# Attention product in halves of TensorE's rows, and a new order of the first units, in a fused attention and mixture-of-depths kernel

## The chip, the cores and the metric

The kernel runs on one core of a Trainium2 chip. A core has TensorE (PE: matmuls, with weight loads as instructions of their own), VectorE (DVE), ScalarE (ACT), GpSimd (POOL) and SyncE (SP), each with its own instruction queue that it works through in order, and 16 DMA engines that move data between HBM, the chip's large memory, and SBUF, the core's own. Matmul results land in PSUM. The engines wait for each other by semaphores. The metric is the device time of one execution in microseconds (us).

## The reference

Inputs are `q`, `k`, `v` of shape (8, 8, 576, 64): 8 batches, 8 heads, 576 positions, head size 64, all float32.

```python
q_s = softmax(q, axis=-1)                       # over the head size
k_s = softmax(k, axis=2)                        # over the positions
kv  = einsum('bhsd,bhse->bhde', k_s, v)         # 64 x 64 for each head
x   = einsum('bhsd,bhde->bhse', q_s, kv)        # then heads side by side: (8, 576, 512)
for b in range(8):
    scores = x[b] @ w_gate                      # one number for each position
    top = argpartition(-scores, 128)[:128]      # the 128 best positions
    xe = x[b, top]
    y  = maximum(xe @ w1, 0) @ w2               # w1: 512 x 1024, w2: 1024 x 512
    out[b] = x[b]
    out[b, top] = xe + sigmoid(scores[top])[:, None] * y
```

So each batch has an attention part over all positions and an MLP over its 128 best ones, and the MLP of a batch can't start before the whole batch's scores are known.

## The kernel before

**Units.** Work is cut into 16 units `s`: a batch has two, of four heads each. The 576 positions lie as 64 groups of 9 over the partitions: a partition holds 5 positions (`R = 5`) or 4 and a zeroed one. For one unit the steps are

- `load`: k, v and q from HBM, six transfers on SP's queue into one of three sets of buffers
- `k_exp`, `q_exp`: exponentials on ScalarE (L195, L202); `v_copy`: v next to a column of ones (L205), on GpSimd in the first units, else on VectorE
- `kv_mm`: k^T v with the column sums of k, 20 matmuls in two column halves of the array (L215); `kv_out`: its reciprocals on VectorE (L224), the copy of the result on ScalarE (L226), and on VectorE one more column, kv times the gate weights `wg` (L228, L229), so that the product gives the score as well
- `q_t`: transposes of exp(q) on TensorE (L239), scaled with the reciprocals as they leave PSUM (L242, "eviction") on ScalarE
- `x_mm`: the product of q and kv (L253); `x_out`: divided by q's sums on VectorE (L266, L267), with the score column (L269); `x_store`: the unit's rows of `out` to HBM on SP's queue

After the second unit of a batch come `score` (L283 to L294, VectorE and GpSimd), `score_row` (the scores as a row, transposed on TensorE, L302, copied by ScalarE, L305 and L307), five `compare` on VectorE (L315, the rank of each position), `pick` (the index list: L335 on VectorE, L339 on TensorE, L343 to L345, and an indirect DMA on GpSimd that gathers the rows `xr`, L347), `gate` (the sigmoid), `turn` (the rows transposed on TensorE, L368, and copied by ScalarE, L370), `mlp1` in eight pieces (L382, each fourth followed by a Relu on ScalarE, L385), `mlp2` in eight pieces (L392) and `finish` (L400, and the indirect store L401).

Each fp32 matmul, not a transpose, stands in the trace as two records with a weight load each: `x_mm` of a unit, 40 matmuls, as 80.

**Order.** The kernel writes down the order itself: the program order is each engine's order. The first four units (`EARLY = 4`) run in a loop of their own, without an MLP; `fill(n)` puts n matmuls of no use in, and `WARM = 20` such matmuls stand at the start. At its end are `gate` and `turn` of batch 0. In each of its steps the `kv_mm` of the next unit is done, so `kv_mm(4)` is too. From step 4 on a step has one unit's attention and, four units behind, half a batch's MLP: eight `pieces` of `mlp1` in even steps and of `mlp2` in odd ones, two after the transposes, one after the next unit's `kv_mm`, four later, and one last. In odd steps `pick` comes after the first two pieces and `turn` before the last one.

The four matmuls of one head pair and position take a quarter of the array each, 64 rows by 64 columns:

```python
QUARTERS = (0, 0), (1, 1), (0, 1), (1, 0)
for h, c in QUARTERS:
    nc.tensor.matmul(out=x[part(c), h, r * C:(r + 1) * C], lhsT=qT[part(h), i, r, c],
                     rhs=kv_w[u % 2][part(h), i], start=True, stop=True)
```

Of the kernel before, what the change touches and what calls it, by code (L numbers as in the profile page):

```python
# [17 lines left out]
def kernel(  # L18
# [24 lines left out]
    R = 5  # L43
# [11 lines left out]
    UP = 2.0 ** 24  # L55
    TINY = 2.0 ** -126
    NV = 5
    WARM = 20
    assert S == 64 * (R + N2) and D == 64 and DM == H * D and DM == 512 and H % 4 == 0
    assert 1 < capacity < S and KF == 8 and NQ == 2  # L60
    assert B * S <= 32 * 256
# [12 lines left out]

    def bank(tag, bufs):
        return ps.tile([P, 512], F32, tag=tag, name=tag, bufs=bufs)


    QUARTERS = (0, 0), (1, 1), (0, 1), (1, 0)

    def part(i):
        return slice(64 * i, 64 * i + 64)
# [38 lines left out]

    wg = const.tile([P, NQ, 2, D], F32, name="wg")
    for h in range(2):
        nc.scalar.dma_start(out=wg[part(h)].rearrange("p a i d -> p (a i) d"),
                            in_=bass.AP(tensor=moe_w_gate.tensor, offset=moe_w_gate.offset + h * D,
                                        ap=[[0, 64], [2 * D, 2 * NQ], [1, D]]))
    warm = const.tile([P, 1], F32, name="warm")
# [65 lines left out]
    def k_exp(u):  # L193
        ke = at.tile([P, 4, R, D], F32, tag="ke", name="ke")
        nc.scalar.activation(out=ke, in_=raw["k"][u % LD], func=AF.Exp)  # L195
        st["ke", u] = ke

    def q_exp(u, i):
        if i == 0:
            st["qe", u] = at.tile([P, 2, R, 2, D], F32, tag="qe", name="qe")  # L200
        qr = raw["q"][u % LD].rearrange("p (i h) r d -> p i r h d", i=2)
        nc.scalar.activation(out=st["qe", u][:, i], in_=qr[:, i], func=AF.Exp)  # L202

    def v_copy(u, engine=nc.vector):
        engine.tensor_copy(out=v_ones[u % 2][:, :, :, :D], in_=raw["v"][u % LD])  # L205
# [22 lines left out]
        nc.vector.tensor_mul(prod, kv[:, :, :D], wg[:, qd])  # L228
        nc.vector.reduce_sum(out=kw[:, :, D + 1], in_=prod, axis=AX.X)  # L229

    def q_t(u, i):

        if i == 0:
            st["qT", u] = at.tile([P, 2, R, 2, D], F32, tag="qT", name="qT")
        qe = st["qe", u] if i == 0 else st.pop(("qe", u))
        t_ps = ps.tile([P, 2, 512], F32, tag="x", name="x", bufs=2)
        for r in range(R):
            for a in range(2):
                nc.tensor.transpose(out=t_ps[:, a, r * 64:(r + 1) * 64],  # L239
                                    in_=qe[part(a), i, r].rearrange("p h d -> p (h d)"),  # L240
                                    identity=ident[part(a), part(a)])
        nc.scalar.activation(out=st["qT", u][:, i].rearrange("p r a c -> p a r c"),  # L242
                             in_=t_ps[:, :, :R * 64].rearrange("p a (r c) -> p a r c", r=R),
                             func=AF.Copy, scale=krec[:, u, i:i + 1])

    def x_mm(u, i):


        qT = st["qT", u] if i == 0 else st.pop(("qT", u))
        x = ps.tile([P, 2, 512], F32, tag="x", name="x", bufs=2)  # L250
        for r in range(R):
            for h, c in QUARTERS:
                nc.tensor.matmul(out=x[part(c), h, r * C:(r + 1) * C], lhsT=qT[part(h), i, r, c],  # L253
                                 rhs=kv_w[u % 2][part(h), i], start=True, stop=True)
        st["x", u, i] = x

    xs, sr = {}, {}

    def x_out(u, i):
        b, qd = units[u]  # L260
        if qd == 0 and i == 0:
            xs[b] = xp.tile([P, R, NQ, 2, 2, D], F32, tag="xs", name="xs")
            sr[b] = md.tile([P, NQ * 2, G], F32, tag="sr", name="sr")
        x = st.pop(("x", u, i))[:, :, :R * C].rearrange("p h (r c) -> p h r c", r=R)
        rec = qrec[:, u, i].rearrange("p (h r) -> p h r", h=2)
        nc.vector.reciprocal(out=rec, in_=x[:, :, :, D])  # L266
        nc.vector.tensor_mul(xs[b][:, :, qd, i].rearrange("p r h d -> p h r d"), x[:, :, :, :D],  # L267
                             rec.to_broadcast([P, 2, R, D]))
        nc.vector.tensor_mul(sr[b][:, 2 * qd + i].rearrange("p (h r) -> p h r", h=2), x[:, :, :, D + 1], rec)  # L269

    def x_store(u):
        b, qd = units[u]
# [7 lines left out]
    def score(b, up=2):  # L280

        raw_s = s_all[:, b]
        nc.vector.reduce_sum(out=raw_s, in_=sr.pop(b).rearrange("p a (h r) -> p r a h", h=2),  # L283
                             axis=AX.XY)
        s = md.tile([P, R], F32, tag="s", name="s")
        nc.vector.tensor_mul(s, raw_s, valid_r[:, up])
        nc.vector.tensor_add(s, s, valid_r[:, 1])
        st["s", b] = s

        left = md.tile([P, R], F32, tag="left", name="left")  # L290
        for c in range(2, NV):
            nc.gpsimd.tensor_copy(out=vals[:, b, :, c], in_=raw_s if c == 2 else left)
            if c < NV - 1:
                nc.gpsimd.tensor_sub(left, raw_s if c == 2 else left, vals[:, b, :, c])  # L294
# [15 lines left out]
    def compare(b, r):  # L310

        if r == 0:
            st["rank", b] = md.tile([P, R], F32, tag="rank", name="rank")
        junk = md.tile([P, RP], BF16, tag="junk", name="junk", bufs=1)
        nc.vector.scalar_tensor_tensor(junk, st["srow", b], st["s", b][:, r:r + 1], not_before[:, r],  # L315
                                       op0=OP.subtract, op1=OP.is_ge, accum_out=st["rank", b][:, r:r + 1])
# [185 lines left out]
    def fill(n):  # L502

        junk_ps = bank("mm", 2)
        for _ in range(n):
            nc.tensor.matmul(out=junk_ps, lhsT=ones_b[:, :P], rhs=ones_b, start=True, stop=True)
# [12 lines left out]

    for s in range(EARLY):  # L520
        q_t(s, 0)
        q_t(s, 1)
        k_exp(s + 1)
        v_copy(s + 1, nc.gpsimd)
        fill(2)
        x_mm(s, 0)
        x_mm(s, 1)
        fill(2)
        if s == 2:
            kv_mm(s + 1)  # L530
            q_exp(s + 1, 0)
            fill(3)
            pick(0)
            x_out(s, 0)
            kv_out(s + 1)
            x_out(s, 1)
            x_store(s)
            q_exp(s + 1, 1)
        else:
            x_out(s, 0)  # L540
            x_out(s, 1)
            x_store(s)
            if s == 1:
                score(0)
            kv_mm(s + 1)
            q_exp(s + 1, 0)
            kv_out(s + 1)
            if s == 1:
                score_row(0)
                for r in range(R):  # L550
                    compare(0, r)
            q_exp(s + 1, 1)
            if s == 3:
                score(1)
        fill(2)
        if s == 0:
            load_w1(0)
            load_w1(1)
        elif s == 1:
            load_w1(2)  # L560
            load_w1(3)
            load(4, "kvq")
            load(5, "kvq")
        else:
            load_w2(s - 2)
            load(s + 4, "kvq")
    each(gate, 0)
    each(turn, 0)

    number = None  # L570
    for s in range(EARLY, NU + LAG):

        mlp_b, odd = divmod(s - LAG, 2)
        piece = mlp2 if odd else mlp1
        f_next = 0

        def pieces(n):
            nonlocal f_next
            for _ in range(n):
                each(piece, mlp_b, f_next)  # L580
                f_next += 1

        here = s < NU
        after = s + 1 < NU
        last = s == NU - 1
        ends = s // 2 if here and odd else None
        compared = s // 2 - 1 if here and not odd else None
        chosen = (s - 3) // 2 if here and odd else B - 1 if s == NU else None
        if here:
            q_t(s, 0)  # L590
            q_t(s, 1)
        if after:
            v_copy(s + 1)
            k_exp(s + 1)
        pieces(2)
        if chosen is not None:
            pick(chosen)
        if here:
            x_mm(s, 0)
            x_mm(s, 1)  # L600
            x_out(s, 0)
            x_out(s, 1)
            x_store(s)
        if last:
            score(ends)
        if after:
            kv_and_exp(s + 1)
        if s + 4 < NU:
            load(s + 4, "kvq")
        pieces(1)  # L610
        if last:
            compared = ends
        if compared is not None:
            score_row(compared)
            for r in range(R):
                compare(compared, r)
        if chosen is not None:
            each(gate, chosen)
        if ends is not None and not last:
            score(ends)  # L620
        pieces(4)
        if odd and mlp_b + 1 < B:
            each(turn, mlp_b + 1)
        pieces(1)
        if odd:
            each(finish, mlp_b)
        if s == NU:
            number = sums_in_range()
# [28 lines left out]
```

## Time and profile before

| | |
|---|---|
| device time, three runs | 218.83, 220.24, 220.49 us, median 220.24 |
| span of the profiled execution | 216.0 us |
| PE busy | 197.5 us (91%) |
| weight loads (PEld) busy | 147.2 us (68%) |
| DVE, ACT, POOL busy | 54%, 41%, 16% |
| L253, the product | 1280 matmul records of 64x64 in 16 units |
| DMA from 9 to 42 us | busy 1.07 of its 16 engines' time, 370 GB/s |
| DMA from 86 to 108 us | 0.73, 232 GB/s |
| first matmul of the MLP | 42.64 us |

A row of the timeline gives start, length, engine, line, operation, what is written from what, the count of merged instructions, and in brackets the idle time before them with what ended it. PE's busy time counts filler as work, and matmuls overlap, so lengths of single ones can't be added up; the distance from one group's start to the next group's start is what a group costs. [...]A wait counts only on the engine that the end of the run hangs on.

### The profile page before, as it was taken

How to read it: one execution, taken by the hardware profiler on the slowest of the kernel's cores; microseconds unless marked ns; L12 is line 12 of the kernel's file. 1: busy time of each engine (PE TensorE's matmuls, PEld its weight loads, DVE VectorE, ACT ScalarE, POOL GpSimd, SP SyncE). 2: the span in 40 equal slices, each digit the busy share in tenths (PEclk: the TensorE clock that was granted, in tenths of full speed). 3: DMA queues.
4: the chain of work that ended last, by engine and by line, in shares of the span. 5: the costliest groups of instructions: out<-in, count | busy, mean ns of one | idle time of the engine just before them, and what ended most of it. 6: DMA issues, size and time to landing. Idle time of an engine off the chain costs nothing. (4 is left out here: it accounts for less than half of the span.)

```text
span 216.0 us, 7090 instructions
## 1 busy us (share of the span) xinstructions
PE 197.5 (91%) x3040; PEld 147.2 (68%) x3040; DVE 116.2 (54%) x359; ACT 88.6 (41%) x146; POOL 34.4 (16%) x78
## 2 busy tenths in 40 slices
PE   5987595999999999999999999999999989999960
PEld 2464462799749975897679776996599548749620
DVE  6552595668726774477626872596358665501010
ACT  2386374763626471746265443536263311211100
POOL 6022402300112012200320023001120112101010
PEclk9999999999999999999999999999999999999996
DMA  5999999999999997958594949421313041101001
GB/s 179 299 356 358 375 398 369 362 392 377 377 384 381 375 344 249 314 157 283 171 320 154 313 133 303 161 82 49 113 52 109 7 156 52 49 3 52 5 5 52
DMA packets 39335, 46.81 MB, mean 217 GB/s; under 512 B 2944, under 2 KB 36736, under 8 KB 39296
## 3 DMA queue, kind: packets, MB, share of 16 engines
q1 hardware_dynamic: 36928, 41.36, 56.4%
q0 software_dynamic: 1280, 4.20, 5.7%
q10 hardware_dynamic: 1088, 0.72, 1.1%
q8 instruction: 26, 0.43, 0.8%
q14 instruction: 13, 0.11, 0.2%
HBM read 34.73 MB, written 11.53 MB: 214 GB/s over the span
## 5 line engine op out<-in xcount | busy, mean ns | idle before, releaser
L382 PE MATMUL mm<-xT,w 128*128 128x128 f32 x512 | 62.1, 278 | 0.0
L382 PEld LDWEIGHTS mm<-xT,w 128*128 128x128 f32 x512 | 58.8, 192 | 2.3 <-ACT xT L370 1.5
L392 PE MATMUL mm<-w,hT 128*128 128x512 f32 x128 | 59.9, 603 | 0.0
L315 DVE SCALAR_TENSOR_TENSOR junk<-srow,s,not_before 128x576 bf16<-128x576 f32 x40 | 32.8, 819 | 8.3 <-ACT srow L307 7.2
L392 PEld LDWEIGHTS mm<-w,hT 128*128 128x128 f32 x128 | 22.5, 190 | 21.2 <-issue 20.4
L267 DVE TENSOR_TENSOR xs<-x,qrec 128x640 f32<-128x640 f32 x32 | 26.4, 825 | 1.1
L242 ACT ACTIVATE qT<-x,krec 128x640 f32<-128x640 f32 x32 | 23.9, 792 | 6.2 <-PE x L239 6.1
L400 DVE SCALAR_TENSOR_TENSOR o<-mm,g,xr 128x512 f32<-128x512 f32 x8 | 6.0, 751 | 37.7 <-PE mm L392 37.7
L202 ACT ACTIVATE qe<-q 128x640 f32<-128x640 f32 x32 | 23.6, 739 | 3.0 <-DMA q<-in_q_dram 2.8
L215 PE MATMUL tp<-v_ones,ke 128*64 128x65 f32 x640 | 22.6, 224 | 2.3 <-issue 2.1
L215 PEld LDWEIGHTS tp<-v_ones,ke 128*64 128x64 f32 x640 | 20.3, 137 | 5.3 <-issue 3.0
L253 PE MATMUL x<-kv_w,qT 64*64 64x66 f32 x1280 | 22.4, 221 | 0.0
L347 POOL DMA_INDIRECT xr<-out_dram,idx x8 | 8.0, 996 | 88.8 <-DVE qrec L266 72.6
L253 PEld LDWEIGHTS x<-kv_w,qT 64*64 64x64 f32 x1280 | 20.2, 134 | 2.6 <-ACT qT L242 0.8
L195 ACT ACTIVATE ke<-k 128x1280 f32<-128x1280 f32 x16 | 20.3, 1270 | 2.8 <-DMA k<-in_k_dram 2.8
L385 ACT ACTIVATE hT<-mm 128x512 f32<-128x512 f32 x16 | 9.5, 596 | 28.7 <-PE mm L382 28.7
L239 PEld LDWEIGHTS x<-ident,qe 64*128 64x128 f32 x320 | 11.7, 139 | 11.6 <-issue 5.0
L239 PE MATMUL x<-ident,qe 64*128 64x64 f32 x320 | 14.5, 229 | 4.9 <-issue 1.4
L266 DVE RECIPROCAL qrec<-x 128x10 f32<-128x10 f32 x32 | 6.9, 215 | 20.7 <-PE x L253 20.7
L401 POOL DMA_INDIRECT out_dram<-o,idx x8 | 10.1, 1269 | 46.8 <-DVE o L400 46.8
L226 ACT COPY kv_w<-tp 128x130 f32<-128x130 f32 x16 | 4.3, 266 | 31.4 <-DVE krec L224 31.4
L370 ACT COPY xT<-mm 128x512 f32<-128x512 f32 x8 | 4.7, 585 | 26.9 <-PE mm L368 26.9
(81 smaller groups left out, 126.0 us busy)
## 6 DMA issues: line engine op xcount, KB each, us to landing
k<-in_k_dram SPq DMA_DIRECT2D x16, 320.0 KB, 7.0
q<-in_q_dram SPq DMA_DIRECT2D x16, 320.0 KB, 6.1
out_dram<-xs SPq DMA_DIRECT2D x16, 320.0 KB, 2.9
v<-in_v_dram SPq DMA_DIRECT2D x15, 320.0 KB, 7.9
k<-in_k_dram SPq DMA_DIRECT2D x16, 256.0 KB, 7.2
q<-in_q_dram SPq DMA_DIRECT2D x16, 256.0 KB, 6.4
out_dram<-xs SPq DMA_DIRECT2D x16, 256.0 KB, 3.2
v<-in_v_dram SPq DMA_DIRECT2D x15, 256.0 KB, 7.7
```

Of the source, the lines that this page charges most:

```text
L195: nc.scalar.activation(out=ke, in_=raw["k"][u % LD], func=AF.Exp)
L202: nc.scalar.activation(out=st["qe", u][:, i], in_=qr[:, i], func=AF.Exp)
L215: nc.tensor.matmul(out=kv[part(h), i], lhsT=ke[:, 2 * i + h, r], rhs=vo[:, 2 * i + h, r], start=(r == 0), stop=(r == N2))
L239: nc.tensor.transpose(out=t_ps[:, a, r * 64:(r + 1) * 64], in_=qe[part(a), i, r].rearrange("p h d -> p (h d)"), identity=ident[part(a), pa ...
L242: nc.scalar.activation(out=st["qT", u][:, i].rearrange("p r a c -> p a r c"), in_=t_ps[:, :, :R * 64].rearrange("p a (r c) -> p a r c", r= ...
L253: nc.tensor.matmul(out=x[part(c), h, r * C:(r + 1) * C], lhsT=qT[part(h), i, r, c], rhs=kv_w[u % 2][part(h), i], start=True, stop=True)
L267: nc.vector.tensor_mul(xs[b][:, :, qd, i].rearrange("p r h d -> p h r d"), x[:, :, :, :D], rec.to_broadcast([P, 2, R, D]))
L315: nc.vector.scalar_tensor_tensor(junk, st["srow", b], st["s", b][:, r:r + 1], not_before[:, r], op0=OP.subtract, op1=OP.is_ge, accum_out=s ...
L382: nc.tensor.matmul(out=h_ps[:, f % 4 * m:(f % 4 + 1) * m], lhsT=w1[:, d, f * P:(f + 1) * P], rhs=xT[:, d, :m], start=(d == 0), stop=(d == ...
L385: nc.scalar.activation(out=hT[:, f - 3:f + 1, :m], in_=h_ps[:, :4 * m].rearrange("p (f c) -> p f c", f=4), func=AF.Relu)
L392: nc.tensor.matmul(out=st["y", b, n][:m], lhsT=st["hT", b, n][:, f, :m], rhs=w2[:, f], start=(f == 0), stop=(f == KF - 1))
L401: nc.gpsimd.indirect_dma_start(out=out_rows[:(b + 1) * S], out_offset=bass.IndirectOffsetOnAxis(ap=idx[:m, :1], axis=0), in_=o[:m], in_off ...
```

## The change

It has five parts. They all aim at the first units, where TensorE waits for others, and at the number of TensorE's instructions.

- **Product in halves.** Two matmuls of 64 rows by 128 columns take the place of four quarters: 40 records a unit, not 80.
- **Evictions on two engines.** In units 0 and 1 the second eviction of `q_t` is done by VectorE.
- **Score columns ahead of scaling.** `x_out` is cut into `x_sums` (reciprocal and score column) and `x_scale`. In unit 1 both `x_sums` and `score(0)` stand ahead of the scaling, and the score row and compares follow.
- **Stores ahead of weights.** Both weights of the MLP are loaded after the store of unit 1, `w1` ahead of unit 4's load and `w2` behind it; `w_gate` moves from ScalarE's queue to GpSimd's, ahead of the identity and the iotas.
- **Steps 4 and 5 ("late").** Unit 4 is no longer prepared in the first loop, nor unit 5 in step 4. `turn(0)` comes right after the product of unit 3, and steps 4 and 5 begin with four pieces of the MLP, then prepare their own unit, then a fifth piece.

```diff
-    WARM = 20
+    WARM = 18
...
-        nc.scalar.dma_start(out=wg[part(h)].rearrange("p a i d -> p (a i) d"),
+        nc.gpsimd.dma_start(out=wg[part(h)].rearrange("p a i d -> p (a i) d"),
...
+        if on_vector:
+            nc.vector.tensor_scalar(to, src, krec[:, u, i:i + 1], None, op0=OP.mult)
+        else:
+            nc.scalar.activation(out=to, in_=src, func=AF.Copy, scale=krec[:, u, i:i + 1])
...
-            for h, c in QUARTERS:
-                nc.tensor.matmul(out=x[part(c), h, r * C:(r + 1) * C], lhsT=qT[part(h), i, r, c],
+            for h in range(2):
+                nc.tensor.matmul(out=x[:, h, r * C:(r + 1) * C],
+                                 lhsT=qT[part(h), i, r].rearrange("p a c -> p (a c)"),
                                  rhs=kv_w[u % 2][part(h), i], start=True, stop=True)
...
-        q_t(s, 1)
-        k_exp(s + 1)
-        v_copy(s + 1, nc.gpsimd)
+        q_t(s, 1, on_vector=s < 2)
+        if s + 1 < EARLY:
+            k_exp(s + 1)
+            v_copy(s + 1, nc.gpsimd)
...
+        elif s == 1:
+            x_sums(s, 0)
+            x_sums(s, 1)
+            score(0)
+            x_scale(s, 0)
+            x_scale(s, 1)
+            x_store(s)
             kv_mm(s + 1)
             q_exp(s + 1, 0)
+            kv_out(s + 1)
+            score_row(0)
+            for r in range(R):
+                compare(0, r)
+            q_exp(s + 1, 1)
+            for n in range(KD):
+                load_w1(n)
+            load(4, "kvq")
+            load_w2(0)
+            load_w2(1)
+            load(5, "kvq")
...
+            each(turn, 0)
             x_out(s, 0)
             x_out(s, 1)
             x_store(s)
...
+            score(1)
+            each(gate, 0)
...
+        if s in late:
+            pieces(4)
+            k_exp(s)
+            v_copy(s)
+            kv_and_exp(s)
+            load(s + 3, "kvq")
+            pieces(1)
+        after = after and s + 1 not in late
...
-        pieces(1)
+        if s not in late:
+            pieces(1)
...
-        pieces(4)
+        if s not in late:
+            pieces(4)
```

More of the change, by code (lines that the diff above doesn't have):

```diff
@@ L76, in bank @@
         return ps.tile([P, 512], F32, tag=tag, name=tag, bufs=bufs)
-    QUARTERS = (0, 0), (1, 1), (0, 1), (1, 0)
     def part(i):
@@ L229, in kv_out, with q_t @@
         nc.vector.reduce_sum(out=kw[:, :, D + 1], in_=prod, axis=AX.X)
-    def q_t(u, i):
+    def q_t(u, i, on_vector=False):
         if i == 0:
@@ L241, in q_t @@
                                     identity=ident[part(a), part(a)])
-        nc.scalar.activation(out=st["qT", u][:, i].rearrange("p r a c -> p a r c"),
-                             in_=t_ps[:, :, :R * 64].rearrange("p a (r c) -> p a r c", r=R),
-                             func=AF.Copy, scale=krec[:, u, i:i + 1])
+        to = st["qT", u][:, i].rearrange("p r a c -> p a r c")
+        src = t_ps[:, :, :R * 64].rearrange("p a (r c) -> p a r c", r=R)
+        if on_vector:
+            nc.vector.tensor_scalar(to, src, krec[:, u, i:i + 1], None, op0=OP.mult)
+        else:
+            nc.scalar.activation(out=to, in_=src, func=AF.Copy, scale=krec[:, u, i:i + 1])
     def x_mm(u, i):
@@ L257, with x_view, x_sums @@
     xs, sr = {}, {}
-    def x_out(u, i):
+    def x_view(u, i):
+        rec = qrec[:, u, i].rearrange("p (h r) -> p h r", h=2)
+        return st["x", u, i][:, :, :R * C].rearrange("p h (r c) -> p h r c", r=R), rec
+    def x_sums(u, i):
         b, qd = units[u]
@@ L263, in x_out, with x_scale @@
             sr[b] = md.tile([P, NQ * 2, G], F32, tag="sr", name="sr")
-        x = st.pop(("x", u, i))[:, :, :R * C].rearrange("p h (r c) -> p h r c", r=R)
-        rec = qrec[:, u, i].rearrange("p (h r) -> p h r", h=2)
+        x, rec = x_view(u, i)
         nc.vector.reciprocal(out=rec, in_=x[:, :, :, D])
+        nc.vector.tensor_mul(sr[b][:, 2 * qd + i].rearrange("p (h r) -> p h r", h=2), x[:, :, :, D + 1], rec)
+    def x_scale(u, i):
+        b, qd = units[u]
+        x, rec = x_view(u, i)
         nc.vector.tensor_mul(xs[b][:, :, qd, i].rearrange("p r h d -> p h r d"), x[:, :, :, :D],
                              rec.to_broadcast([P, 2, R, D]))
-        nc.vector.tensor_mul(sr[b][:, 2 * qd + i].rearrange("p (h r) -> p h r", h=2), x[:, :, :, D + 1], rec)
+    def x_out(u, i):
+        x_sums(u, i)
+        x_scale(u, i)
     def x_store(u):
@@ L528 @@
         fill(2)
-        if s == 2:
+        if s == 0:
+            x_out(s, 0)
+            x_out(s, 1)
+            x_store(s)
+            kv_and_exp(s + 1)
+            fill(2)
+        elif s == 1:
[4 more added lines that the diff above has]
+            x_scale(s, 1)
+            x_store(s)
             kv_mm(s + 1)
             q_exp(s + 1, 0)
-            fill(3)
+            kv_out(s + 1)
[9 more added lines that the diff above has]
+            load(5, "kvq")
+        elif s == 2:
+            kv_mm(s + 1)
+            q_exp(s + 1, 0)
+            fill(2)
             pick(0)
@@ L538 @@
             q_exp(s + 1, 1)
+            load(6, "kvq")
         else:
+            each(turn, 0)
             x_out(s, 0)
@@ L542 @@
             x_store(s)
[L543 to L568, printed above, removed]
+            score(1)
+            each(gate, 0)
+    late = EARLY, EARLY + 1
     number = None
@@ L607 @@
             kv_and_exp(s + 1)
-        if s + 4 < NU:
+        if after and s + 4 < NU:
             load(s + 4, "kvq")
-        pieces(1)
+        if s not in late:
+            pieces(1)
         if last:
```

## The prediction

> **What bounds the kernel now.** I read the page's table of slices and groups first, then the chain of waits, then TensorE's (PE's) timeline of the first 75 us, then the other engines beside it. The end of the run is a chain of matmuls, L392 and L382, up to 208.8 us, and from 42.6 to 208.8 us PE is busy 164.6 of 166.2 us. So from the first MLP matmul (L382 at 42.64) on, every PE microsecond and every PE wait moves the end; before it PE runs attention and filler and waits a lot. The change works in that first part, in units 4 and 5, and in each unit's product.
>
> ```profile
> 17.73 0.34 PE L239 MATMUL x<-ident,qe 64*128 64x64 f32 x4 [0.21 <-ACT qe L202]
> 19.42 0.40 PE L239 MATMUL x<-ident,qe 64*128 64x64 f32 x6 [1.35 <-issue]
> ...
> 22.16 1.32 PE L215 MATMUL tp<-v_ones,ke 128*64 128x65 f32 x37
> 25.56 0.33 PE L215 MATMUL tp<-v_ones,ke 128*64 128x65 f32 x3 [2.09 <-issue]
> ...
> 41.24 0.60 PE L368 MATMUL mm<-ident,xr 128*128 128x128 f32 x4
> 41.77 0.84 PE L239 MATMUL x<-ident,qe 64*128 64x64 f32 x20
> 42.64 2.05 PE L382 MATMUL mm<-xT,w 128*128 128x128 f32 x16
> 44.62 1.40 PE L253 MATMUL x<-kv_w,qT 64*64 64x66 f32 x80
> 45.95 1.39 PE L215 MATMUL tp<-v_ones,ke 128*64 128x65 f32 x40
> ...
> 55.96 0.27 PE L339 MATMUL tp<-vals,hit 128*128 128x5 bf16 x5
> 56.16 1.43 PE L253 MATMUL x<-kv_w,qT 64*64 64x66 f32 x80
> 57.53 1.41 PE L215 MATMUL tp<-v_ones,ke 128*64 128x65 f32 x40
> 58.86 4.56 PE L392 MATMUL mm<-w,hT 128*128 128x512 f32 x10
> 63.26 0.60 PE L368 MATMUL mm<-ident,xr 128*128 128x128 f32 x4
> ```
>
> Two things are to be seen. PE stands still in the middle of a run of like matmuls for 1.35 and 2.09 us, and nothing is named but issue: it is out of instructions. And around 42 and 56 us each wait of another engine is covered: the transposes L239 cover ScalarE's copy of xT, and ten L392 records (4.3 us) stand between the selection L339 and L368, the transposes of the rows it gathers. That gather takes long there, as its own view (tile xr, from 55 to 66 us) says, and the weight loads of L368 did wait for it, though no matmul did:
>
> ```profile
> PEld mm L368: 0.5, 1
> ...
> DMA to landing us min/median/max: 6.2/6.2/6.2
> ```
>
> For batch 2, with the queues less full, it is 3.9.
>
> [...]80 records of 64x64 (four tiles, L253) go by in 1.33 us from start to next start, 40 of 128x64 (two tiles, L215) in 1.32. [...]L239 loads 64x128 for each record, and 20 of them take 0.77 us, 38 ns each[...]. [...]The page's instruction queue shows 26 packets and 0.43 MB, 16.5 KB each.
>
> **The change, part by part.**
>
> Product: 80 records of a quarter become 40 of 64x128. Two halves run at once where four quarters did, each record streaming the same 66 columns. By L215's rate 40 records take 1.32 us[...]. Against 1.33 that is 0 to +0.07 us a unit, 0 to 0.8 in the 12 units after the MLP starts. I take 0.03 a unit, 0.3 to 0.4 in all. It does halve the product's instructions, which matters where instructions come late. The two stalls lie 127 pairs of load and matmul apart (6 + 2 + 80 + 2 + 37 in the timeline)[...], and PE went on at 19.4 and 25.6 us[...]. I take 0.1 us for what is left of 1.35 + 2.09.
>
> The gate weights on GpSimd's queue: two issues ahead of ident and the iotas. GpSimd's indirect issues last 0.97 us (L347) to 1.27 (mean of L401); a direct one is not in the trace. I take 1.0 each (bounds 0 and 1.3). VectorE waits for the first iota (until 2.93) and is busy without a break to its v copy, 7.50 to 8.32; all that comes 2.0 later, to 10.3. Unit 0's kv product goes from 9.22 to 10.4. On ScalarE the second exp(q) stands behind the kv copy, which waits for that product, so the second transposes end at 13.6 and the eviction on VectorE at 14.4: it saves nothing here. Two warm-up matmuls less are covered by the wait for v. Product of unit 0: 13.0 to 14.1.
>
> Unit 1: without the 1.35 stall and with the second eviction (0.79) on VectorE, the product goes from 20.3 to 19.6. Unit 2's kv product can't start before its v has landed and been copied (20.33 + 1.25 = 21.6; it was 22.16), and then runs through without 2.09. Score column ahead of scaling: s at 22.1 instead of 24.05, VectorE then scales until 23.7, kv_out(2), row of scores; compares from 24.95 instead of 27.39. From there the spacing stays: pick, gather issued at 31.4 instead of 33.97. Store 1 lands ahead of that. Gather in full queues, 6.2: 37.6. PE is at turn(0) by 36.9 (kv product of unit 4 and two fillers moved behind it). So turn(0) goes from 41.24 to **37.6**: 3.6 us won. The sum is little moved by the 2.0 at GpSimd, as v of unit 2 lands when it does.
>
> Then what stands behind it, by the order in the built program. After turn(0) the MLP follows at once: the xT copy, until then covered, is waited for: +1.40 from turn(0) as before but with nothing in 0.87 of it. MLP 39.0. Four pieces (32 records at 0.111) to 42.6. ScalarE has their Relu (0.60) ahead of exp(k) of unit 4 (1.27), and the kv product waits for both: **1.9**, to 44.5. Kv 1.33, piece 0.99, q_t 0.87, two pieces 1.98: product of unit 4 at 49.7. Product, score row, piece: L392 from 52.5, four pieces to 56.0. VectorE: x_out until product + 0.88 + 2.13 = 52.7, five compares (4.2) to 56.9, and only then v's copy for unit 5 (0.82): kv product at 57.8, **1.8** waited. To pick(1) 1.33+0.95+0.9+1.75: 62.7. Gather issued 0.94 later as before, 63.65. But the five L392 pieces are spent: between pick and turn(1) stand only product and kv product, PE is there at 65.6. The gather lands after 3.9 to 6.2 us. Unit 8's loads are still moving then, and 9's come behind a store: I take 5.1, 68.75, **3.1** waited. Turn(1) at 68.8 instead of 63.26: +5.5. Cross-check: -3.6 + 1.33 (kv product moved) + 0.87 + 1.9 + 1.8 + 3.1 = +5.4. From turn(1) on the order is the old one, PE-bound, so the delay goes to the end: +5.5 + 0.3 = about 5.6, and 220.24 becomes **225.8**.
>
> Edits that cost nothing: the loads' new order (w1 is the end of the same set of transfers as before, lands near 34, used from 39.0; w2 near 45, used at 52.5), x_sums before x_scale within a unit (same VectorE work, the tail's score still after both).
>
> **Rivals.** (1) The head start wins: the waits in units 4 and 5 are hidden. Then 3.6 less the moved kv product, 2.3 us: 218. For it: VectorE and ScalarE are only half busy (54%, 41%), and fetches get rarer. Against: each wait is in one in-order queue behind named work, and no spare PE work stands behind the waiter. (2) Even: the gather needs 3.9 (-1.2) and the head start is larger, turn(0) at 36.3, if v of unit 2 lands earlier and GpSimd's delay is hidden (-1.3); 5.6 less 2.5 leaves +3.1, and one of the waits of 1.8 or 1.9 must go too: about 221.4. For it: both gather times are in the trace. Against: the order in front of the last two waits is fixed. (3) Weight loads of 128 columns bound the halves: [...]+1 us a unit, about 12 on top: 238. L239 speaks against it.
>
> **Numbers.** Forecast 0.72, rival 1 0.14, rival 2 0.09, rival 3 0.05. Unknown costs in the forecast: gather 3.9 to 6.2 (-1.2/+1.1), GpSimd (-0.6/+0.3), arrival of v in unit 2 (0.7), a clock drop[...]. That alone is 223.5 to 228.5; down to rival 2 and a little below, 218.8 to 229, leaves out most of rival 1 and rival 3. Faster 0.14, same 0.10, slower 0.76.
>
> **What would show it.** Matmuls of the product 40 a unit, about 1.3 us from start to next start; no issue stall of over 0.5 us on PE in units 1 and 2; GpSimd's first iota near 4.8; turn(0) near 37.6; then PE idle: 1.9 released by ScalarE's ke, 1.8 by VectorE's v copy, 2 to 4 by the DMA of xr. Wrong if turn(0) comes before 35, if the xr wait is missing, or if the product takes over 1.6.

## The result and the profile after

The changed kernel takes **246.06 us** (median; 245.03 to 251.68) against 220.0 us of the kernel before in the same measurement: ratio **1.118**, 95% interval 1.111 to 1.124. The forecast was 225.8 with a range up to 229.0, so the direction was right and the size was not: +26 us came where +5.6 was expected. The execution of 251.68 us, at a lower granted clock than the other three (0.928 against 0.950 to 0.952), is left out of the ratio.

First the page: TensorE's busy share in 40 equal slices of the span, and the clock it was granted in tenths, in the profile after. In the kernel before the clock row is 9 up to the last slice.

```profile
PE   6889796888979999999999999999999989979970
...
PEclk9999866579999999999999999999999999999996
```

The clock falls in slices 5 to 9, 24 to 55 us. The clock's own record in the trace puts it at half speed from 28.3 to 35.2 and from 38.6 to 52.2 us, 20.5 us in all ahead of the end.

Then TensorE's timeline (start, duration, line, tile, count, and in brackets the idle time ahead and what ended it):

```profile
20.04 2.45 PE L252 MATMUL x<-kv_w,qT 64*128 64x66 f32 x40
...
22.96 1.39 PE L212 MATMUL tp<-v_ones,ke 128*64 128x65 f32 x40
...
25.84 0.32 PE L313 MATMUL tp<-ident,s 128*128 128x128 f32 x1 [0.91 <-DVE prod L225]
...
28.09 4.35 PE L252 MATMUL x<-kv_w,qT 64*128 64x66 f32 x40
...
33.34 2.21 PE L212 MATMUL tp<-v_ones,ke 128*64 128x65 f32 x40
...
35.92 0.27 PE L350 MATMUL tp<-vals,hit 128*128 128x5 bf16 x5
...
37.85 0.53 PE L236 MATMUL x<-ident,qe 64*128 64x64 f32 x10 [1.66 <-DVE krec L221]
...
41.21 4.54 PE L252 MATMUL x<-kv_w,qT 64*128 64x66 f32 x40
...
46.51 1.06 PE L379 MATMUL mm<-ident,xr 128*128 128x128 f32 x4
48.24 5.73 PE L393 MATMUL mm<-xT,w 128*128 128x128 f32 x32 [0.68 <-ACT xT L381]
55.81 1.39 PE L212 MATMUL tp<-v_ones,ke 128*64 128x65 f32 x40 [1.85 <-ACT ke L192]
...
69.94 1.39 PE L212 MATMUL tp<-v_ones,ke 128*64 128x65 f32 x40 [1.50 <-DVE v_ones L202]
...
75.10 2.45 PE L252 MATMUL x<-kv_w,qT 64*128 64x66 f32 x40
77.48 1.39 PE L212 MATMUL tp<-v_ones,ke 128*64 128x65 f32 x40
79.35 0.66 PE L379 MATMUL mm<-ident,xr 128*128 128x128 f32 x4 [0.48 <-DMA xr<-out_dram,idx]
```

The reader sees three things. The product (L252) goes on for 2.38 us from its start to the next, 75.10 to 77.48, where the quarters took 1.33; the one at 41.21, at half clock, lasts 4.54. The two stalls of before (1.35 and 2.09, released by issue) are gone, as foretold. They are called fetch stalls here, a reading from the times: in the trace of before one packet of the instruction queue (q8) moves ahead of the end of each, between 16.8 and 18.2 us and between 22.9 and 24.2, and TensorE goes on at 19.42 and 25.56; the page counts 26 of these packets before and 21 after. And the waits on exp(k), on the copy of v and on xT stand where they were foretold, with 1.85, 1.50 and 0.68 us; the wait for the second gather is 0.48 instead of 3.1.

Cut at the same two places, the traces compare as follows (spans 216.0 and 243.7 us; the first is of an execution of 217.89 us, one of the quicker ones, so the difference is 27.7 here and 26.1 between the medians):

| stretch | before | after | more |
|---|---|---|---|
| start to first MLP matmul | 42.64 | 48.24 | 5.6 |
| from there to turn(1), the second gather's transposes | 20.62 | 31.11 | 10.5 |
| from there to the end | 152.74 | 164.35 | 11.6 |

The last stretch holds ten products: 10 x 1.05 = 10.5 of its 11.6. The middle one holds two (2.1), the three waits on TensorE (1.85 + 1.50 + 0.48 = 3.8), the kv product and the transposes of unit 4 that stood ahead of the MLP before (1.32 + 0.84), and the MLP's first 32 records at partly half clock (5.73 against 3.84 in the runs below where the clock stays full, 1.9): 10.0 of 10.5. So the product costs 12 x 1.05 = 12.6 of the 27.7 us between the two traces. What it is made of, and why the clock fell, the experiments had to show.

### The profile page after: what moved, and what is told of

It reads as the page before. It is cut to its first block, busy times and chain, and to the rows that moved or that the text cites. A ratio compares the mean times of both kernels' runs of the same rounds, so it can differ in the third digit from the quotient of the medians.

```text
span 243.7 us, 5783 instructions
## 1 busy us (share of the span) xinstructions
PE 220.1 (90%) x2385; PEld 170.2 (70%) x2391; DVE 120.3 (49%) x362; ACT 87.1 (36%) x144; POOL 34.8 (14%) x79
## 5 line engine op out<-in xcount | busy, mean ns | idle before, releaser
L393 PE MATMUL mm<-xT,w 128*128 128x128 f32 x512 | 64.2, 283 | 0.7 <-ACT xT L381 0.7
L393 PEld LDWEIGHTS mm<-xT,w 128*128 128x128 f32 x512 | 60.7, 197 | 3.2 <-ACT xT L381 2.4
L252 PE MATMUL x<-kv_w,qT 64*128 64x66 f32 x640 | 43.2, 292 | 0.0
L252 PEld LDWEIGHTS x<-kv_w,qT 64*128 64x128 f32 x640 | 40.9, 205 | 3.0 <-ACT qT L244 1.3
L212 PEld LDWEIGHTS tp<-v_ones,ke 128*64 128x64 f32 x640 | 20.9, 142 | 8.0 <-issue 4.0
L244 ACT ACTIVATE qT<-x,krec 128x640 f32<-128x640 f32 x30 | 22.4, 790 | 5.8 <-PE x L236 5.8
L412 POOL DMA_INDIRECT out_dram<-o,idx x8 | 9.9, 1236 | 44.4 <-DVE o L411 44.3
```

The lines of the kernel that those rows point to most:

```text
L212: nc.tensor.matmul(out=kv[part(h), i], lhsT=ke[:, 2 * i + h, r], rhs=vo[:, 2 * i + h, r], start=(r == 0), stop=(r == N2))
L244: nc.scalar.activation(out=to, in_=src, func=AF.Copy, scale=krec[:, u, i:i + 1])
L252: nc.tensor.matmul(out=x[:, h, r * C:(r + 1) * C], lhsT=qT[part(h), i, r].rearrange("p a c -> p (a c)"), rhs=kv_w[u % 2][part(h), i], star ...
L393: nc.tensor.matmul(out=h_ps[:, f % 4 * m:(f % 4 + 1) * m], lhsT=w1[:, d, f * P:(f + 1) * P], rhs=xT[:, d, :m], start=(d == 0), stop=(d == ...
L412: nc.gpsimd.indirect_dma_start(out=out_rows[:(b + 1) * S], out_offset=bass.IndirectOffsetOnAxis(ap=idx[:m, :1], axis=0), in_=o[:m], in_off ...
```

## The experiments

Ratios are to the kernel before, on the same chip. That kernel's median was 224.0, 224.6 and 219.4 us on the three chips that were used, and no trace of it was taken there, so a comparison of ratios from different chips holds to about 2% only; where it matters, traces are compared.

### The product: load or streaming

Halves alone, in the kernel before:

```diff
-            for h, c in QUARTERS:
-                nc.tensor.matmul(out=x[part(c), h, r * C:(r + 1) * C], lhsT=qT[part(h), i, r, c],
+            for h in range(2):
+                nc.tensor.matmul(out=x[:, h, r * C:(r + 1) * C],
+                                 lhsT=qT[part(h), i, r].rearrange("p a c -> p (a c)"),
```

> The kernel before with the product in halves and nothing else of the change. Theory A, the product itself is the larger part of the loss: a pair of 64x128 records goes by in 112 ns as in the changed kernel, 2.4 us a unit and not 1.33, so 12 units behind the start of the MLP give +13 us and the first four up to 4 more: 233 to 238 us. If the half clock of the changed kernel (28 to 52 us) came from the product, the clock falls here too and it is 240 or more. Rival B, the product only looks slow because of the new order around it: 220 to 223 us.

Measured: 233.81 us, ratio 1.047 (1.039 to 1.054). A product lasts 2.45 us; within it the matmul records start in pairs, 7 and then 105 ns apart, so a pair comes every 112 ns; in the quarters four records come every 58.5 ns. Both fetch stalls are gone. The MLP begins at 46.58, and from there to the end the trace takes 185.4 us where the kernel before takes 173.4: 12.1 more, with the old order. The ratio is worth 9.8 us only, as the kernel before takes longer on this chip. So this one part makes the product slow. The clock is at half from 34.7 to 44.9 us, after waits of 1.21 and 1.13 us that the trace of the kernel before has too, without a fall; whether the halves bring the clock down, this run does not show.

The same halves with twice the columns streamed by each matmul (the second 66 are the same numbers again, and fall where the next matmul overwrites them, or beyond what is read):

```diff
-                                 rhs=kv_w[u % 2][part(h), i], start=True, stop=True)
+                nc.tensor.matmul(out=x[:, h, r * C:(r + 2) * C].rearrange("p (n c) -> p n c", n=2), ...
+                                 rhs=kv_w[u % 2][part(h), i][:, None].to_broadcast([64, 2, C]), ...
```

> The kernel before with the product in halves, each half streaming its 66 columns twice (132), the second copy into the place that the next position overwrites, so the same loads and twice the stream. Theory L, the load of 128 fp32 weight columns sets the 112 ns of a pair: [...]the product stays at 2.4 to 2.5 us a unit and the time equals that of halves alone. Rival S, the two halves' streams run one after the other: 220 ns a pair, 4.6 us a unit, some 26 to 35 us more than halves alone.

Measured: 232.38 us (one run), and a pair still every 112 ns. Doubling what is streamed costs next to nothing (2.46 us from a product to what follows, where it was 2.38): the weight load sets the pace. A group by line of this run between 80 and 200 us:

```profile
L253 PE MATMUL x<-kv_w,qT 64*128 64x132 f32 x360 | 22.7, 277 | 0.0
```

The mean of one record is 277 ns; it was 275 with 66 columns.

Twice the loads, each for 33 columns (two matmuls for each one of the halves):

```diff
+            for n in range(2):
+                for h in range(2):
+                    nc.tensor.matmul(out=x[:, h, r * C + n * C // 2:r * C + (n + 1) * C // 2], ...
+                                     rhs=kv_w[u % 2][part(h), i, n * C // 2:(n + 1) * C // 2], ...
```

> The kernel before with the product in halves, each half cut into two matmuls of 33 columns: twice the loads, the same stream. Theory L: 40 pairs a unit at 112 ns, 4.5 to 4.7 us a unit, 25 to 35 us more than halves alone. Rival S: half the stream for each record, 56 to 60 ns a pair, 2.4 to 2.6 us a unit, about the time of halves alone.

Measured: 284.17 us (one run), 80 records in 4.66 us, again 112 ns a pair. The number of loads sets the time; the columns streamed do not.

The opposite test, in the kernel before: the transposes of q as ordinary matmuls with the identity.

```diff
-                nc.tensor.transpose(out=t_ps[:, a, r * 64:(r + 1) * 64], ...
-                                    identity=ident[part(a), part(a)])
+                nc.tensor.matmul(out=t_ps[:, a, r * 64:(r + 1) * 64], ...
+                                 rhs=ident[part(a), part(a)], start=True, stop=True)
```

> The kernel before with the transposes of exp(q) as ordinary fp32 matmuls with the identity: 40 records of the same 64x128 weights and 64 columns and not 20. Theory L: as an ordinary matmul each load takes what it takes in the halves of the product, 20 pairs at about 112 ns, 2.3 us a unit and not 0.77, so the transposes were no measure for the product. Rival T: the load is the same in both, 20 pairs at 62 ns, 1.3 to 1.4 us a unit.

Measured: 251.34 us (one run). TensorE's timeline of it, the same work of one unit as the x20 rows of L239 in the kernel before:

```profile
91.13 2.45 PE L239 MATMUL x<-ident,qe 64*128 64x64 f32 x40
93.51 1.98 PE L392 MATMUL mm<-w,hT 128*128 128x512 f32 x4
```

Twenty transposes of 0.77 us became 40 records and 2.38 us, with the same tiles and the same data. So the transposes were no measure for the product: an ordinary fp32 matmul leaves two records where a transpose leaves one, and each load is dearer (192 ns against 139 below). That could have been seen in the weight-load groups of the kernel before (80 to 200 us; busy time and mean ns of one load):

```profile
L382 PEld LDWEIGHTS mm<-xT,w 128*128 128x128 f32 x370 | 42.5, 192 | 1.9 <-ACT xT L370 1.3
...
L253 PEld LDWEIGHTS x<-kv_w,qT 64*64 64x64 f32 x655 | 10.4, 134 | 0.6
...
L239 PEld LDWEIGHTS x<-ident,qe 64*128 64x128 f32 x160 | 5.6, 139 | 3.5 <-ACT xT L370 3.0
```

A 128-column load of an ordinary matmul lasts 192 ns there, one of 64 columns 134, and the transposes' load of 128 columns 139, like one of 64. TensorE's timeline of the kernel before has the two kinds one behind the other:

```profile
48.81 4.63 PE L382 MATMUL mm<-xT,w 128*128 128x128 f32 x40
53.37 0.84 PE L239 MATMUL x<-ident,qe 64*128 64x64 f32 x20
54.14 1.98 PE L392 MATMUL mm<-w,hT 128*128 128x512 f32 x4
```

From start to next start that is 0.114 us a record for L382 and 0.038 for L239. In the kernel after, the product's load has moved to the first kind:

```profile
L252 PEld LDWEIGHTS x<-kv_w,qT 64*128 64x128 f32 x400 | 23.1, 188 | 0.7
```

### The new order without the halves

The changed kernel with the product in quarters again:

```diff
-            for h in range(2):
-                nc.tensor.matmul(out=x[:, h, r * C:(r + 1) * C], ...
+            for h, c in QUARTERS:
+                nc.tensor.matmul(out=x[part(c), h, r * C:(r + 1) * C], lhsT=qT[part(h), i, r, c], ...
```

> The changed kernel with the product in quarters again, all else of the change kept. Theory A: product back at 1.33 us a unit; what is left are the waits in units 4 and 5 (0.7 for xT, 1.9 for exp(k), 1.5 for the v copy, 1 to 3 for the gathered rows): 224 to 227 us with a full clock. If the order of the first units itself lets the clock fall to half as in the changed kernel, 8 us more: 232 to 235. Rival B: stays above 240.

Measured: 231.36 us, ratio 1.032 (1.027 to 1.037): 7.3 us for all the rest of the change. Its middle stretch, cut as in the table, is 28.39 us against 20.62, 7.8 more, so the cost lies there. Its timeline of TensorE:

```profile
19.73 0.34 PE L238 MATMUL x<-ident,qe 64*128 64x64 f32 x4 [1.34 <-issue]
...
26.27 0.22 PE L214 MATMUL tp<-v_ones,ke 128*64 128x65 f32 x1 [0.95 <-issue]
...
41.41 0.67 PE L380 MATMUL mm<-ident,xr 128*128 128x128 f32 x4 [0.30 <-DMA xr<-out_dram,idx]
42.75 3.84 PE L394 MATMUL mm<-xT,w 128*128 128x128 f32 x32 [0.68 <-ACT xT L382]
```

The fetch stalls are back with the quarters, so it was the number of instructions that made them. The first gather is used at 41.41, where the kernel before has 41.24: the head start of 3.6 us isn't there. The clock was at half from 21.0 to 24.4 and from 38.1 to 41.5 us.

The first units' order alone, with the quarters, with units 4 and 5 as before and the gate weights on ScalarE's queue again (from the run above):

```diff
-        nc.gpsimd.dma_start(out=wg[part(h)].rearrange("p a i d -> p (a i) d"),
+        nc.scalar.dma_start(out=wg[part(h)].rearrange("p a i d -> p (a i) d"),
...
-        if s + 1 < EARLY:
-            k_exp(s + 1)
-            v_copy(s + 1, nc.gpsimd)
+        k_exp(s + 1)
+        v_copy(s + 1, nc.gpsimd)
...
-            each(turn, 0)
             x_out(s, 0)
             x_out(s, 1)
             x_store(s)
+            kv_and_exp(s + 1)
             score(1)
+            fill(2)
+            load(7, "kvq")
             each(gate, 0)
+            each(turn, 0)
...
-    late = EARLY, EARLY + 1
+    late = ()
```

> The kernel before with the order of the first four units from the changed kernel (second eviction on VectorE, score ahead of scaling, stores ahead of weights), but quarters, the gate weights on ScalarE's queue, unit 4 prepared in the first loop and steps 4 and 5 as before. Theory A: the loss that is left with quarters lies in steps 4 and 5, so this is within 1% of the kernel before, or up to 3 us faster: the compares start 1 to 3 us earlier. Rival B, the order of the first units costs by itself: 2 us or more slower than before.

Measured: 230.19 us, ratio 1.028 (1.021 to 1.035), turn(0) at 44.31. Moving the kv product of unit 4 back ahead of turn(0) removes the wait on exp(k), and turn(0) comes later. One wait of 1.59 us stays, at 50.68: VectorE's copy of v for unit 5 waits 3.81 us for its transfer and ends at 50.5, as that load now stands behind w2. So the first units' order costs by itself. How much of that is the clock is open: it was at half for 13.7 us ahead of the end of this trace, and its mean over the four executions was 0.957 to 0.963, where the kernel before had 0.972 to 0.987 on this chip.

The run of the new order in quarters with both waits taken away (exp(k) ahead of the Relus, the copy of v for unit 5 on GpSimd):

```diff
         if s in late:
-            pieces(4)
             k_exp(s)
-            v_copy(s)
+            pieces(4)
+            v_copy(s, nc.vector if s == EARLY else nc.gpsimd)
```

> The changed kernel with quarters, and with two of the waits in steps 4 and 5 taken away: exp(k) of units 4 and 5 ahead of the four MLP pieces (and so ahead of their Relu) on ScalarE, and the v copy of unit 5 on GpSimd and not behind the compares on VectorE. Theory A: each wait is on the path that ends last, 1.85 + 1.75 us, so 3 to 4 us less than quarters with all waits (231.4 beside 224.0). Rival B: the time is made up elsewhere, above all by a longer wait for the gathered rows of batch 1: less than 1.5 us won.

Measured: 231.73 us, ratio 1.033 (1.025 to 1.040), nothing won. Both waits are gone, and one of the same size stands behind them:

```profile
70.06 0.66 PE L380 MATMUL mm<-ident,xr 128*128 128x128 f32 x4 [3.13 <-DMA xr<-out_dram,idx]
```

It was 0.43 in the run with both waits, and turn(1) at 71.14. The gather of batch 1 was the next bound; the two waits only stood in front of it, and hid it.

### The clock

The changed kernel with filler matmuls in the waits of the first units: if these waits bring the clock down, it stays up here. Nobody reads what the filler computes.

```diff
+        if s == 3:
+            fill(6)
         q_t(s, 0)
+        fill((1, 1, 2, 5)[s])
         q_t(s, 1, on_vector=s < 2)
...
             score_row(0)
+            fill(4)
```

> The changed kernel as it is, product in halves, with matmuls of no use in the places where TensorE waits in the first four units (1, 1, 2 and 5 between the two halves of the transposes, 6 ahead of unit 3's, 4 behind the row of scores). Theory C: the clock falls to half[...], so this holds it up: half clock for 7 us at most and not 20.5, and 5 to 9 us less than the changed kernel, 237 to 241. Rival D: the clock falls for another reason, or the filler delays work: 244 to 248.

Measured: 237.97 us, ratio 1.060 (1.052 to 1.067), with the same waits later on (0.68, 1.85, 1.50, 0.46). The page's clock row:

```profile
PEclk9999999979999999999999999999999999999998
```

The changed kernel once more, on another chip:

> The changed kernel as it is, on the chip of the three runs that follow, so that each of them differs from it by one thing. If the chip is like the others: ratio 1.10 to 1.12 to the kernel before, product 2.4 us a group, TensorE's clock halved for 14 to 21 us of the first 75. If the ratio falls below 1.09, part of the loss of the first measurement was of that chip and not of the change.

Measured: 242.9 us, ratio 1.108 (1.101 to 1.116), half clock from 36.8 to 50.4 us:

```profile
PEclk9999995589999999999999999999999999999997
```

Filler, which does no work, makes the kernel faster: the three executions with a trace span 243.7 and 240.8 us without it (20.5 and 13.7 us at half clock ahead of the end) and 236.2 with it (3.4 us). So the clock is worth about 4.6 to 7.5 us of the change. These traces are not all from one chip; but if work takes at most twice as long at half clock (the product took 4.54 us at it and 2.45 at full clock, 1.85 times), 17.1 and 10.2 us less of it save at most 8.5 and 5.1, which fits.

What lowers the clock? The stretches in its record are about 3.4 us long or a multiple of that (3.41, 6.83 and 13.65 us between the first fall and the last rise in the trace of the changed kernel). In every trace here but one, each fall ahead of the end follows 3.4 us in which TensorE was idle for 1.2 to 2.8 us, in one or several waits: 1.56 and 1.91 us ahead of the two falls of the changed kernel (those of 0.91 and 1.66 us in its timeline among them), 2.56 ahead of the one in its other trace. Filler takes the waits of the first units away, and the falls there with them; the one fall that is left, at 50.0, follows the wait of 1.85. Idle time alone doesn't decide, as stretches with up to 1.8 us of it pass without a fall. Nor is it needed. In the run with 33 columns for each load the clock drops again and again:

```profile
PE   6999996999999999999999999999999999989990
...
PEclk9979777589988999799979999899979997999996
```

Ahead of the end it is at half clock for 44.4 us. One of its falls comes at 113.6 us:

```profile
108.84 4.66 PE L254 MATMUL x<-kv_w,qT 64*128 64x33 f32 x80
113.43 2.33 PE L215 MATMUL tp<-v_ones,ke 128*64 128x65 f32 x40
```

Nine of its ten falls follow 3.4 us without any idle time on TensorE, like this one, and the later ones among them come when the product has filled nearly all of it. So the clock can fall while TensorE is busy. Whether it falls because few columns are streamed is not shown: the product with 33 columns also lasts 4.6 us, longer than 3.4, and with 66 or 132 columns only about 2.4, so columns and length change together. With 66 columns (halves alone) the clock was at half for 10.2 us and with 132 for 3.4, but each time after 1.7 to 1.8 us of waits, so this pair says nothing about the columns. In the changed kernel all three falls that were traced follow waits.

### Order and clock apart

The changed order with the filler and with quarters (both diffs are above):

> The changed order with the product in quarters and with filler matmuls in the waits of the first units. Theory (three separate costs: product 1.05 us in each of 12 units behind the first MLP, clock, order): the product's 12 to 13 us go against the filler run in halves (1.06), and the clock's 4 to 5 us against the quarters without filler (1.032): ratio 1.005 to 1.015, half clock under 4 us before the end, turn(0) near 41. Rival ([...]the filler only takes up time): 1.03, half clock 8 us or more.

Measured: 228.88 us; the ratio of 1.037 (1.028 to 1.047) rests on the quickest two executions, 226.4 and 227.9 us. The ratio is the rival's and the clock the theory's: it stayed up (half only from 73.6 to 77.0 us ahead of the end), but the time did not come back. The execution with the trace took 229.9 us:

```profile
26.65 0.33 PE L213 MATMUL tp<-v_ones,ke 128*64 128x65 f32 x3 [2.61 <-issue]
...
42.76 0.63 PE L379 MATMUL mm<-ident,xr 128*128 128x128 f32 x4 [1.64 <-DMA xr<-out_dram,idx]
44.06 3.84 PE L393 MATMUL mm<-xT,w 128*128 128x128 f32 x32 [0.68 <-ACT xT L381]
...
73.33 0.89 PE L379 MATMUL mm<-ident,xr 128*128 128x128 f32 x4 [2.36 <-DMA xr<-out_dram,idx]
```

Here the fetch stall (0.95 without filler) is 2.61, and the gathers keep TensorE waiting for 1.64 and 2.36. In the two quicker executions these waits may be shorter; no trace of them was taken. By the ratio the order costs about 8 us (6 to 10) with the clock mostly up, at a mean of 0.982 and 0.993 in these two. From the first MLP matmul to the end the trace takes 183.6 us and the halves with filler 193.3; the quarters wait 1.9 more for the second gather, so the product makes 9.7 + 1.9 = 11.6 of the 12.6 us worked out above.

The kernel before with the filler, and with the score columns ahead of the scaling as well (the second diff is that run alone):

```diff
+        if s == 3:
+            fill(6)
         q_t(s, 0)
+        fill((1, 1, 2, 5)[s])
         q_t(s, 1)
```

```diff
-            x_out(s, 0)
-            x_out(s, 1)
-            x_store(s)
+            x_sums(s, 0)
+            x_sums(s, 1)
             if s == 1:
                 score(0)
+            x_scale(s, 0)
+            x_scale(s, 1)
+            x_store(s)
```

> The kernel before with the same filler, nothing else of the change. Its runs on these chips had mean clocks of 0.966 to 0.989, while the profile of the first measurement had full clock up to the end. Theory: the first units' waits of the kernel before also let the clock fall in some executions, and the filler takes that away: ratio 0.985 to 0.995, mean clock 0.985 or more. Rival: the filler stands in front of work that was ready, and the time is the same or up to 2 us longer: 1.00 to 1.01.

> The kernel before with the filler and one part of the change: in the first two units the reciprocals and score columns of both halves ahead of the scaling. Theory (from turn(0) on TensorE is the bound, so an earlier selection is worth its whole lead): VectorE's two scalings of 0.8 us move behind the score of batch 0, turn(0) comes 1.0 to 1.6 us earlier than in the run with the filler alone, and the time falls by as much: 0.5% less. Rival (the gather lands when the queues let it): the gather starts earlier and lands at the same time, no difference to the filler alone.

Measured: ratios 1.004 (1.000 to 1.007) and 1.003 (1.000 to 1.005); the rival held both times, and no version that was tried beats the kernel before. Why an earlier score wins nothing is plain in the second of them, first on TensorE, then on VectorE:

```profile
25.63 0.49 PE L215 MATMUL tp<-v_ones,ke 128*64 128x65 f32 x5 [2.39 <-issue]
26.05 1.44 PE L313 MATMUL tp<-ident,s 128*128 128x128 f32 x5
```

```profile
22.50 0.17 DVE L298 TENSOR_TENSOR s<-s,valid_r 128x5 f32<-128x5 f32 x1
...
27.93 0.82 DVE L326 SCALAR_TENSOR_TENSOR junk<-srow,s,not_before 128x576 bf16<-128x576 f32 x1 [0.65 <-ACT srow L318]
```

The score is there at 22.7, against 24.05 in the kernel before. But its transposes (L313) stand on TensorE behind the kv product of unit 2, which stalls for 2.39 us on issue, and start at 26.05; the comparisons start at 27.93, against 27.39. With the filler alone the score is there at 23.9, and still the transposes start at 26.13 and the comparisons at 28.01. On TensorE's queue the fetch stall, and not the score, is what ends last there.

## Why the prediction was wrong

The direction was right, and so was one mechanism (waits in units 4 and 5, covered by nothing); but all four waits together make 4.5 of the 27.7 us, and most of the loss came from elsewhere. The step that failed is the product: "I take 0.03 a unit, 0.3 to 0.4 in all", an estimate of the author's from L215's rate and from L239's 38 ns for each record with a load of 64x128. It measured 1.05 us a unit, 12.6 in all. A second term, the clock, had been left without a size. Point by point:

- **Product.** The rival at 238 us (the 128-column loads as the bound, "+1 us a unit") had the right mechanism and size and got 0.05. It was put aside because L239 loads 64x128 in 38 ns. Neither row of the estimate was a measure: L239 is a transpose, and L215 loads 64 columns. A row of the right kind stood in the same trace: L382, ordinary matmuls with 128 columns of weights, at 0.114 us a record. At that pace, an estimate, 20 pairs take 2.28 us where the quarters take 1.33, about 1 us more a unit. The runs agree: 112 ns a pair, with 66, 132 or 33 columns streamed. The 20 transposes take 2.38 us as ordinary matmuls against 0.77, 3.1 times as long; the loads of 192 against 139 ns in the kernel before already spoke against L239 as a measure.
- **Fetch stalls**, 1.35 + 2.09 to 0.1: right, though the 0.1 was the author's estimate. No issue stall over 0.33 us is left on TensorE, and the stalls return with the quarters.
- **GpSimd's issues.** Two took 1.50 us together where 2.0 was assumed; the first iota came at 4.26 instead of 4.8, the kv product of unit 0 at 9.95 instead of 10.4, the product at 13.53 instead of 14.1.
- **The head start**, turn(0) at 37.6: wrong. It was 46.51 and 43.24 in the two executions of the changed kernel, 41.41 in quarters, 41.56 with filler. Unit 2's kv product began at 22.96, not at 21.6, because the product of unit 1 ahead of it ended late; the comparisons began at 26.44, not at 24.95. Then the clock halved: the selection (L350) had its input from VectorE at 31.6, but stood on TensorE behind a product of 4.35 us and a kv product of 2.21, until 35.92. In quarters the comparisons started at 27.97, behind the fetch stall, and the gather took 7.1 us and not 6.2.
- **The waits** of 0.87, 1.9 and 1.8: 0.68, 1.85 and 1.50, right. The wait of 3.1 for the second gather was 0.48: the gather took 3.5 us instead of the assumed 5.1, and the longer product covered another 1.05. In the run where the two waits ahead of it were taken away it was 3.13.
- **The clock.** It stood among the unknown costs ("a clock drop") without a size. It cost 4.6 to 7.5 us, and no long wait came before it: the longest gap on TensorE between 9 us and the first fall at 28.3 was 0.9 us. Several short ones within 3.4 us had gone before it, 1.56 us together. The stretches at half clock lasted 3.4, 6.8 and 13.7 us in the traces.

The sum between the two traces: product 12.6, clock 7.5, which leaves 7.6 of 27.7 for the order (7.3 in the run with quarters in the changed kernel). The split of clock and order is an estimate, as the 7.5 is a difference of two traces and the quarters' run lost some clock too. The order's 5.2 us in the prediction was near, but by luck: the head start of 3.6 and the second gather's wait of 3.1 are both missing, and these misses nearly cancel.

Still open is why the kernel before takes 219 us on one chip and 224 on others: no trace of it was taken there. The clock is not the reason: its mean was alike, 0.980 and 0.978 (medians) on the two slower chips and 0.978 on the quicker. More stalls of the fetch may be part of it: the four traces of kernels with quarters from the slower chips have 1.5 to 2.2 us of issue stalls on TensorE after 50 us, the three from the quicker chip 0 to 0.7.

## What to carry to other kernels

Price a new matmul shape by a row of the same kind (ordinary or transpose, same type, same columns of weights), and look at the weight-load rows as well as at the matmul rows; here a tile with twice the columns and half the instructions took 2.38 us a unit instead of 1.33. Where two rows of a trace seem to give different prices (here L382 with 0.114 us and L239 with 0.038 us a record, both with 128 columns of weights), ask what differs between them before one is put aside. Give every cost that is named a size, or a bound, the clock too. Before an operation is moved forward, look up what else its user stands behind on the in-order queue.

## What the runs showed of the hardware

- An ordinary fp32 matmul with 128 columns of weights on one half of the rows leaves records that come at 112 ns a pair, whether 33, 66 or 132 columns are streamed; four quarters of 64 columns had come at 58.5 ns.
- An fp32 transpose with a 64x128 load took 0.77 us for 20, and the same work as ordinary matmuls 2.38.
- The granted clock fell to half after 3.4 us with 1.2 to 2.8 us of idle time on TensorE, in waits of which in the changed kernel ahead of the first fall none was over 0.9 us. In the run with 33 columns a load nine of ten falls came after 3.4 us without idle time.
- Direct DMA issues on GpSimd took 0.75 us each (two in 1.50), the first two gathers in the same trace, which are indirect, 1.07 and 1.03.
- Filler that saves 4.6 us or more in the changed kernel, where the clock falls, was worth nothing in the kernel before (1.004).
